# An attention and MLP kernel: a first product in three passes, another written-out order, and GpSimd additions tied to other VectorE operations

## The chip, the cores and the metric

The kernel runs on one core of one Trainium2 chip. The metric is the device time of one execution in microseconds (us); the median of three runs of the kernel before is 1144.4 us.

## What is computed

The input x has 2048 rows of 640 values. Four layers follow one another, each added to x: attention, MLP, attention, MLP, with the same weights both times.

- Attention: y = layernorm(x), qkv = y·wqkv (640×1920), 32 heads of 20 values. Each row looks at 8 rows: itself and the rows 2, 4, ..., 14 before it. Logits q·k/√20, softmax over the 8, weighted sum of v, product with wo (640×640).
- MLP: y = layernorm(x), h = gelu(y·w1 + b1) with 1536 columns, then h·w2 + b2.

```python
logits = einsum("bhsd,bhswd->bhsw", q, kg) * scale      # 8 keys a row
o = einsum("bhsw,bhswd->bhsd", softmax(logits), vg)
x = x + o @ wo
x = x + gelu(layernorm(x) @ w1 + b1) @ w2 + b2
```

## The kernel before

**Tiling.** The rows are split by parity and then in halves: four units of 512 rows, each of M = 4 tiles of 128 rows. Unit numbers 0 to 3 are the first pair of layers, 4 to 7 the second. All products are made from float16 pairs: a float32 value is split into a high half (a cast, on ScalarE) and a low half (the difference, on VectorE), and TensorE adds up three passes, high·high, high·low and low·high. The weights are scaled by 64 and split in the same way while the kernel runs; wqkv is prepared in four head groups g of three pieces (q, k, v): a ScalarE operation makes the high piece (L434), a VectorE operation the low one (L435), out of a staging buffer that a DMA has filled (L447).

**The stages of a unit.** Layer norm (for units 0 and 1 with VectorE statistics L561 to L563, a GpSimd power L566 and a VectorE scaling L606; for the others ScalarE sums, a GpSimd power L590 and ScalarE scalings); the split in high and low halves (L613 ScalarE, L615 VectorE); the transposition (by DMA, L620; for tiles 0 and 1 of unit 0 by TensorE into PSUM, L489, with a ScalarE copy back, L497); 16 products with wqkv of 15 matmuls of 480 columns (L654; tile t, head group g), each evacuated by ScalarE (L673) and stored to DRAM; then, for each head group, the gathered rows are loaded and VectorE makes products q·k (L741), sums them to logits (L745, a reduction over 20 values), softmax (L750 to L760), products with v (L767) and their sums (L775, L779). GpSimd makes the low half of the attention's output (L788). Then the product with wo (L810), the residual on VectorE (L816), the second layer norm, the addition of b2 to x on GpSimd (L624), the MLP's products (L847, L866, L869; in other forms L1024, L1061, L1124 for the last units), GELU on ScalarE, splits on VectorE (L858), residuals (L889, L1143).

**What sets the order.** The program first lists all operations with what they need, give and use (numbered in the order in which they are listed), and emits them in an order written out by hand: `ORDER` is that list of numbers. `PLACES` says which buffer of its pool each tenant gets. Each engine runs its operations in the order of emission; SyncE (SP) issues all DMAs in that order too. Waits come from the data alone, by buffers. In addition `BESIDE` names 49 GpSimd additions (L624 and L788) and for each a VectorE operation that it waits for (L1204). The `need` of an operation makes no wait by itself: it is an argument for whoever makes the order.

**Around the change.** TensorE's queue begins with nine groups of eight matmuls of 128 columns (L1153), which multiply a unit matrix with itself into a bank that nobody reads. Their listing names the first tile's statistics as a need. The product of tile 0 with head group 0 is cut into three passes of five matmuls (L661): high·high, low·high, high·low. That of tile 1 is one run of 15 (L654).

Of the kernel before, what the change touches and what calls it, by code (L numbers as in the profile page):

```python
# [261 lines left out]
def sliding_dilated_then_mlp_kernel(  # L262
# [141 lines left out]
    def identity():  # L404
# [7 lines left out]
        give=["b1"])  # L412
# [822 lines left out]
```

## Time and profile before

| | |
|---|---|
| median of 3 runs (lowest, highest) | 1144.4 us (1144.36, 1145.14) |
| profiled execution: its time, its span | 1144.26 us, 1142.5 us |
| TensorE (PE) busy | 1134.2 us, 99% |
| VectorE (DVE) busy | 1073.7 us, 94% |
| ScalarE (ACT) busy | 552.5 us, 48% |
| GpSimd (POOL) busy | 159.1 us, 14% |
| mean granted TensorE clock | 0.998 |

The span runs from the first instruction to the last; 1.76 us of the execution's time lie around it. A matmul's shown duration is longer than its share of the stream, since matmuls are pipelined: what counts for TensorE is the distance from one start to the next. The rows of the trace on which the prediction rests stand in a section of their own below. In them PE is TensorE's matmuls, PEld its weight loads, DVE VectorE, ACT ScalarE, POOL GpSimd.

### The profile page before, as it was taken

Reading aid. Unit: us, or ns where it says so; the run is one execution under the profiler, and the core shown is the slowest. Engines: PE = TensorE matmul, PEld = TensorE weight load, DVE = VectorE, ACT = ScalarE, POOL = GpSimd, SP = SyncE. Lnnn points to the kernel's source line nnn. Section 1 sums busy time; section 2 is a strip of 40 time slices with the busy share of each in tenths; the row PEclk is TensorE's granted clock in tenths of the full one; section 3 lists DMA queues with packets and bytes.
Section 4 is the critical chain, followed back from the end, with each engine's and each line's share of the span. In section 5 each row is a group of like instructions: output and inputs, shape, how many; then the busy total and the mean of one; then the engine's idle time right before and its main releaser. Section 6 shows DMA issues by size and latency. Waiting matters only on the chain.

```text
span 1142.5 us, 17648 instructions
## 1 busy us (share of the span) xinstructions
PE 1134.2 (99%) x6932; PEld 647.0 (57%) x6932; DVE 1073.7 (94%) x1003; ACT 552.5 (48%) x977; POOL 159.1 (14%) x98
## 2 busy tenths in 40 slices
PE   8999999999999999999999999999999999999998
PEld 5444446577654565445555654556455546566886
DVE  8899999999999999999999999999999999988482
ACT  5476434545364438423645552355447542286360
POOL 2011110311111113100213011121211200300000
PEclk9999999999999999999999999999999999999999
DMA  9999999899976675956475866674598877788856
GB/s 295 324 311 277 278 331 279 262 266 308 240 198 196 216 192 125 253 182 188 155 216 188 179 188 188 213 190 133 164 267 275 258 209 221 211 218 225 251 152 189
DMA packets 259023, 257.38 MB, mean 225 GB/s; under 512 B 138540, under 2 KB 209532, under 8 KB 258940
## 3 DMA queue, kind: packets, MB, share of 16 engines
q1 hardware_dynamic: 258940, 256.26, 78.0%
q8 instruction: 54, 0.88, 0.3%
q14 instruction: 29, 0.24, 0.1%
HBM read 175.64 MB, written 48.71 MB: 196 GB/s over the span
## 4 chain that ended last, share of the span: by engine, by line
PE 99%; DVE 0%; DMA 0%; issue 0%
PE ps L654 34%; PE ps L847 17%; PE acc L866 14%; PE ps L810 11%; PE acc L1124 9%; PE ps L1061 7%; PE acc L869 4%; PE acc L1024 3%; PE ps L1024 1%; PE acc L1153 0%; DMA xf<-in_A_x_dram 0%; PE ps L661 0%; DVE bn L561 0%; PE acc L489 0%; DVE hl L615 0%; DVE bn L562 0%
## 5 line engine op out<-in xcount | busy, mean ns | idle before, releaser
L654 PE MATMUL ps<-wq,yT 128*128 128x480 f16 x1905 | 390.4, 366 | 0.0
L654 PEld LDWEIGHTS <-yT 128*128 128x128 f16 x1905 | 185.6, 98 | 197.0
L847 PE MATMUL ps<-yT,c 128*128 128x512 f16 (+1 forms) x1080 | 204.0, 344 | 0.0
L866 PE MATMUL acc<-c,act 128*128 128x512 f16 x720 | 203.4, 379 | 0.0
L741 DVE TENSOR_TENSOR pr<-qk 128x2560 f32<-128x2560 f32 (+1 forms) x44 | 179.6, 4088 | 0.7
L767 DVE TENSOR_TENSOR pr<-sm,v 128x2560 f32<-128x2560 f32 (+1 forms) x44 | 177.1, 4032 | 0.4
L745 DVE TENSOR_REDUCE sm<-pr 128x128 f32<-128x2560 f32 (+1 forms) x44 | 176.6, 4017 | 0.0
L847 PEld LDWEIGHTS <-c 128*128 128x128 f16 x1080 | 103.8, 98 | 87.4
L673 ACT ACTIVATE ev<-ps 128x480 f32<-128x480 f32 x128 | 70.7, 564 | 162.9 <-PE ps L654 155.5
L869 PE MATMUL acc<-c,act 128*128 128x128 f16 x720 | 148.2, 219 | 0.0
L775 DVE TENSOR_TENSOR pr<-pr 128x2560 f32<-128x2560 f32 (+2 forms) x88 | 143.8, 1645 | 0.2
L810 PE MATMUL ps<-wo,yT 128*128 128x320 f16 x960 | 134.7, 299 | 0.0
L866 PEld LDWEIGHTS <-act 128*128 128x128 f16 x720 | 70.3, 98 | 80.3 <-DVE act L858 0.2
L810 PEld LDWEIGHTS <-yT 128*128 128x128 f16 x960 | 93.0, 98 | 38.1
L590 POOL TENSOR_TENSOR ln<-ln,half 128x2 f32<-128x2 f32 (+1 forms) x30 | 48.6, 1621 | 408.9 <-ACT ln L587 408.9
L1124 PE MATMUL acc<-c,wq 128*128 128x320 f16 x630 | 92.9, 299 | 0.0
L853 ACT ACTIVATE act<-ps,b 128x512 f32<-128x512 f32 (+1 forms) x72 | 43.8, 613 | 93.1 <-PE ps L847 56.0
L624 POOL TENSOR_TENSOR xf<-xf,b 128x640 f32<-128x640 f32 x28 | 58.1, 2085 | 172.9 <-DVE xf L816 36.0
L788 POOL TENSOR_TENSOR ohl<-o,ohl 128x640 f16<-128x640 f32 x24 | 44.3, 1846 | 266.6 <-ACT ohl L786 118.7
L1061 PE MATMUL ps<-yT,c 128*128 128x512 f16 x360 | 78.7, 379 | 0.0
L1124 PEld LDWEIGHTS <-wq 128*128 128x128 f16 x630 | 61.6, 98 | 24.2
L571 ACT ACTIVATE junk<-xf 128x640 f16<-128x640 f32 x56 | 41.1, 733 | 66.8 <-DVE xf L816 54.8
(137 smaller groups left out, 1145.1 us busy)
## 6 DMA issues: line engine op xcount, KB each, us to landing
c<-mw SPq DMA_DIRECT2D x180, 320.0 KB, 4.0
spill<-ev SPq DMA_DIRECT2D x64, 480.0 KB, 5.6
qk<-spill SPq DMA_DIRECT2D x32, 880.0 KB, 5.4
v<-spill SPq DMA_DIRECT2D x32, 880.0 KB, 5.7
c<-msp SPq DMA_DIRECT2D x36, 320.0 KB, 3.6
qk<-spill SPq DMA_DIRECT2D x32, 320.0 KB, 4.8
c<-mw SPq DMA_DIRECT2D x54, 160.0 KB, 3.1
mw<-c SPq DMA_DIRECT2D x24, 320.0 KB, 5.6
```

The costliest lines, as they stand in the source:

```text
L654: nc.tensor.matmul(ps, transposed(yk)[:, a * KD + k, t * P:(t + 1) * P], wq[:, b, k, g], start=j == 0, stop=j == 3 * KD - 1)
L673: act(3 * GC, -400 + n, lambda i=i, pk=pk, ek=ek: nc.scalar.activation(tile_of(*ek)[:, :, i], tile_of(*pk)[:, :3 * GC].rearrange("p (a c) ...
L741: return nc.vector.tensor_mul(pr(pk), w[:, HALO + m + t0:HALO + m + t0 + TH, None, :].to_broadcast([P, TH, W, GC]), windows(w, t0, [GC, W] ...
L745: dve(E, G - 0.7, lambda pk=pk, t0=t0: nc.vector.tensor_reduce(lg(t0, t0 + TH).rearrange("p t w h -> p (t w h)"), pr(pk).rearrange("p t w ...
L767: return nc.vector.tensor_mul(pr(vk).rearrange("p t w (h d) -> p t (w h) d", d=DH), lg(t0, t0 + TH).rearrange("p t w h -> p t (w h)")[:, : ...
L775: dve(TH * w * GC, G - 0.9, lambda vk=vk, w=w: nc.vector.tensor_add(pr(vk)[:, :, 0:w], pr(vk)[:, :, 0:w], pr(vk)[:, :, w:2 * w]), need=[la ...
L810: nc.tensor.matmul(tile_of(*pk)[:, :D // 2], transposed(yk)[:, a * KD + k, t * P:(t + 1) * P], wo[:, b, k, c * D // 2:(c + 1) * D // 2], s ...
L847: nc.tensor.matmul(tile_of(*pk)[:, :nt], tile_of(*ck)[:, a, k * P:(k + 1) * P], transposed(yk)[:, c * KD + k, t0 * P:t1 * P], start=i == 0 ...
L866: nc.tensor.matmul(acc[i], w, tile_of(*wk)[:, c, :BANK], start=e == 0 and (a, c) == PASS[0], stop=end, skip_group_check=True)
L869: nc.tensor.matmul(acc[4][:, i * P:(i + 1) * P], w, tile_of(*wk)[:, c, BANK:], start=e == 0 and i == t0 and (a, c) == PASS[0], stop=end, s ...
L1061: nc.tensor.matmul(tile_of(*pk), tile_of(*ck)[:, a, k * P:(k + 1) * P], transposed(yk)[:, c * KD + k, :], start=i == 0, stop=i == 3 * KD - 1)
L1124: nc.tensor.matmul(acc[bank][:, :HD], tile_of(*hk)[half][:, a, slot, t * P:(t + 1) * P], load()[:, z, c], start=q in FIRST and i == 0 and ...
```

## The change

Four edits, all of them about order and waits; no matmul, addition or transfer is added to the whole or taken from it.

1. The product of tile 1 with head group 0 in unit 0 is cut in three passes of five matmuls as well (two list entries more, so that all later numbers grow by 2).
2. The nine groups of L1153 no longer name the statistics as a need.
3. `ORDER` and `PLACES` are replaced as a whole.
4. `BESIDE` is replaced: each addition waits for another VectorE operation. In the old table the next VectorE operation after the one waited for is a sum of logits (L745) in 19 of 49 cases, in the new one in 47 of 49.

```diff
-                if n == 0 and g == 0 and t == 0:
+                if n == 0 and g == 0 and t in (0, 1):
                     def part(a, b, t=t, g=g, pk=pk):
...
-                           give=[("qkvp", n, t, g) if c else ("qkvq", a)], use=[pk, yk])
-                        last = [("qkvq", a)]
+                           give=[("qkvp", n, t, g) if c else ("qkvq", t, a)], use=[pk, yk])
+                        last = [("qkvq", t, a)]
...
     for _ in range(WARM):
-        warm([("sq", ("a", 0), 0)])
+        warm([])
...
 ORDER = """
-1 11 0 12 13 15 21 18 33 14 35 26 34 63 28 41 36 37 29 42 72 16 31 43 38 91 22 44 48 46 55 66 19 27 17 32 56 30 69 20 49 24 25 45 57 51 47 50 213 58
+0 11 1 12 13 30 15 25 28 27 21 24 32 26 84 33 29 31 18 35 34 14 41 36 37 42 91 16 44 43 69 38 22 48 46 45 55 66 49 23 56 63 50 51 19 57 53 52 39 213
...
 BESIDE = {
-    278: 298, 302: 649, 326: 163, 395: 403, 400: 538, 405: 555, 410: 724, 497: 203, 520: 533, 543: 552, 607: 778, 612: 778, 617: 802, 622: 802,
...
+    280: 135, 304: 139, 328: 342, 397: 405, 402: 2046, 407: 2128, 412: 1067, 499: 512, 522: 535, 545: 2106, 609: 781, 614: 781, 619: 802, 624: 802,
...
```

Read by engine, the two orders begin as follows (hi and lo are halves; yT is a transposed tile's copy; wqh and wql are the high and the low piece of wqkv, head group and piece; t is the tile of unit 0; "turn" a transposition on TensorE; "pass" five matmuls of L661).

```
TensorE before: 4 groups L1153, turn t0 hi, turn t0 lo, 5 groups L1153, turn t1 hi,
                pass t0 hi.hi, turn t1 lo, pass t0 lo.hi, pass t0 hi.lo, t1 (15, L654), t2, (t0, g1), t3, ...
TensorE after:  9 groups L1153, turn t0 hi, turn t0 lo, turn t1 hi, turn t1 lo,
                t0 hi.hi, t1 hi.hi, t0 lo.hi, t1 lo.hi, t0 hi.lo, t1 hi.lo, t2, (t0, g1), t3, ...
ScalarE before: hi t0, wqh 0,0, wqh 0,2, wqh 0,1, hi t2, hi t1, yT t0 hi, yT t0 lo, yT t1 hi, wqh 1,0, yT t1 lo, ...
ScalarE after:  hi t0, wqh 0,0, wqh 0,2, yT t0 hi, hi t1, hi t2, wqh 0,1, yT t1 hi, yT t1 lo, yT t0 lo, hi t3,
                wqh 1,0, wqh 1,2, wqh 1,1, ...
VectorE before: statistics t0, t1, y t0, statistics t2, lo t0, y t1, y t2, wql 0,0, wql 0,1, lo t2, lo t1, wql 0,2, statistics t3, ...
VectorE after:  statistics t0, t1, y t0, statistics t2, lo t0, y t1, y t2, wql 0,2, lo t1, lo t2, statistics t3, wql 0,0, wql 0,1,
                y t3, statistics of a tile of unit 1, lo t3, wql 1,0, wql 1,2, wql 1,1, ...
SP before:      x t0, t1, t2, w 0,0, w 0,2, w 0,1, x t3, w 1,0, w 2,0, ...
SP after:       x t0, t1, t2, w 0,0, w 0,2, w 3,1, w 0,1, x t3, ...
TensorE's end before: ..., 3 runs of "p4", "p3" mixed; last a run of p3 (tile 1); VectorE's last residual and the last output DMA follow it
TensorE's end after:  all p4 before the last five runs of p3; last the same run of p3, the same residual and output DMA
```

## Rows read from the trace of the kernel before

**Rows 1.** The page: busy us and share by engine; one group (busy us, mean ns).

```profile
PE 1134.2 (99%) x6932; PEld 647.0 (57%) x6932; DVE 1073.7 (94%) x1003; ACT 552.5 (48%) x977; POOL 159.1 (14%) x98
...
L654 PE MATMUL ps<-wq,yT 128*128 128x480 f16 x1905 | 390.4, 366 | 0.0
```

**Rows 2.** All waits of TensorE: for whom, us in total, times, longest.

```profile
PE acc L489 <- ACT hl L613: 2.8, 1, 2.8
PE acc L1153 <- POOL ident L406: 1.4, 1, 1.4
PE acc L489 <- DVE hl L615: 0.7, 1, 0.7
```

**Rows 3.** Stretches: TensorE's busy us (count), granted clock, DMA share, GB/s.

```profile
1.00:5.00 4.00, 3.60 (x32) 1.00 0.78 248
5.00:8.90 3.90, 0.45 (x5) 1.00 1.08 305
8.95:12.30 3.35, 3.32 (x32) 0.50 1.11 348
12.40:16.40 4.00, 4.00 (x39) 1.00 1.37 310
500.00:700.00 200.00, 200.00 (x1182) 1.00 0.64 182
```

**Rows 4.** Timeline of the head, TensorE: start us, us, what, count.

```profile
1.35 3.60 PE L1153 MATMUL acc<-ident 128*128 128x128 f16 x32 [1.35 <-POOL ident L406]
7.79 0.45 PE L489 MATMUL acc<-ident,hl 128*128 128x128 f16 x5 [2.84 <-ACT hl L613]
8.98 0.72 PE L489 MATMUL acc<-ident,hl 128*128 128x128 f16 x5 [0.74 <-DVE hl L615]
9.49 3.76 PE L1153 MATMUL acc<-ident 128*128 128x128 f16 x40
13.36 1.18 PE L661 MATMUL ps<-wq,yT 128*128 128x480 f16 x5
16.68 23.66 PE L654 MATMUL ps<-wq,yT 128*128 128x480 f16 x116
```

**Rows 5.** Timeline of the head, ScalarE and VectorE.

```profile
3.90 0.89 DVE L561 BATCH_NORM_STATS2 bn<-xf 128x6 f32<-128x320 f32 x2 [3.04 <-DMA xf<-in_A_x_dram]
9.13 0.87 ACT L434 ACTIVATE wq<-pr 128x800 f16<-128x800 f32 x1 [0.44 <-DMA pr<-in_A_wqkv_dram]
10.40 0.87 ACT L434 ACTIVATE wq<-pr 128x800 f16<-128x800 f32 x1 [0.40 <-DMA pr<-in_A_wqkv_dram]
11.18 1.35 ACT L613 ACTIVATE hl<-y 128x640 f16<-128x640 f32 x2
12.43 1.87 ACT L497 ACTIVATE yT<-acc 128x640 f16<-128x640 f16 x3
17.26 0.61 DVE L606 TENSOR_SCALAR y<-xf,bn 128x640 f32<-128x640 f32 x1 [0.44 <-POOL bn L566]
19.02 0.83 DVE L615 TENSOR_TENSOR hl<-y,hl 128x640 f16<-128x640 f32 x1
19.77 1.89 DVE L435 SCALAR_TENSOR_TENSOR wq<-ohl,wq 128x800 f16<-128x800 f32 x2
```

**Rows 6.** One line's instructions on GpSimd: count, min/median/max ns, first and last start.

```profile
L624 POOL TENSOR_TENSOR xf<-xf,b x28: 1536/1549/6722, 217.5 to 990.6; 128x640 f32<-128x640 f32 x28
...
L788 POOL TENSOR_TENSOR ohl<-o,ohl x24: 1387/1402/4557, 99.0 to 986.1; 128x640 f16<-128x640 f32 x24
```

**Rows 7.** Groups of VectorE by shape: count, busy us, mean ns, idle before.

```profile
L741 DVE TENSOR_TENSOR pr<-qk 128x5120 f32<-128x5120 f32 x20 | 109.8, 5489 | 0.4
...
L745 DVE TENSOR_REDUCE sm<-pr 128x256 f32<-128x5120 f32 x20 | 109.4, 5470 | 0.0
L741 DVE TENSOR_TENSOR pr<-qk 128x2560 f32<-128x2560 f32 x24 | 69.8, 2922 | 0.2
L767 DVE TENSOR_TENSOR pr<-sm,v 128x2560 f32<-128x2560 f32 x24 | 67.3, 2820 | 0.1
...
L858 DVE TENSOR_TENSOR act<-act 128x512 f16<-128x512 f32 x48 | 35.3, 737 | 0.6 <-ACT act L856 0.6
```

**Rows 8.** Timeline about two additions beside other VectorE operations.

```profile
598.38 5.48 DVE L741 TENSOR_TENSOR pr<-qk 128x5120 f32<-128x5120 f32 x1
598.54 8.68 POOL L624 TENSOR_TENSOR xf<-xf,b 128x640 f32<-128x640 f32 x2 [19.18 <-DVE sm L760]
603.78 2.03 DVE L858 TENSOR_TENSOR act<-act 128x512 f16<-128x512 f32 x1
```

**Rows 9.** Timeline at a narrow place in the middle.

```profile
358.10 0.68 DVE L858 TENSOR_TENSOR act<-act 128x512 f16<-128x512 f32 x1
...
358.83 0.10 PEld L866 LDWEIGHTS <-act 128*128 128x128 f16 x1 [0.17 <-DVE act L858]
```

**Rows 10.** Timeline of the end.

```profile
1137.83 1.25 PE L1124 MATMUL acc<-c,wq 128*128 128x320 f16 x8
...
1139.12 0.49 DVE L1143 SCALAR_TENSOR_TENSOR xf<-acc,xf 128x320 f32<-128x320 f32 x1 [0.32 <-PE acc L1124]
```

More of the change, by code (lines that the diff above doesn't have):

```diff
@@ L71 @@
 ORDER = """
[111 rows of a table removed]
[111 rows of a table added]
 """
 PLACES = """
-000000000110000110101032320001111220230203102102132000110303222011120003200121102220011202120002200001001000110100001011000001110010221012110201100111
-010110011012022101012122011201022001001000001100010010010000011001020120120002110100121210001102101202010121202111002200000100100001100100001100001101
-000102112021120011001010100011011212000121202000200112000010010000011010000100100001101012020101220011001102011101001211202021210101021210201000100100
-000110100001001000011010210201210002110001100011001102201102001222010101221020001001000001101000010010000110100012200121000111100111111000020011202120
@@ L190 @@
-101022100011200010010000011010000100100001101011220021000101111002010110011021210100220112001211201000100100000110100001001000011010220010221200212301
-132012012112000002021102002111002021102002111102020102012111002021102012111000002021102002111102020102012111002021102002111102000102112111100000020201
-020121100020211020022111010201020122111010201020022101000000101010201221100101110200221110102010201221210101010201211200000002011102002112102010102012
-112002011102112112002001102202110100000020101222120100010111222020101010101222120100010111222020001102210011102220011232100041212150001100022002100120
@@ L194 @@
-02110022100020211101021212100023211114020205100102002011020020110221100220200011010110000022220200311010140000025200211000022010010220110220
+000000000110000110101302100302111320220001112220130103020020111322020321200121102210021102210022000100100000110001000000010011000110112021210211001101
+011100110110100122210102021210102001001000000111000000100100110100012012012002011110020211011002201000121202010211120020000100100011000100100100001101
+000101212011020110011000110011002100222011120002102220000100010000011010000100100001101012121120021000110012010110011210120201012222012100122000100100
@@ new lines @@
+000110100001001000011010202010211002011001101000110011101002201120012220111000001001000001101000010010000110100120011201101010110111111000021102210021
+012200121212000010010000011010000100100001101011200021201110000102111001001201210120201110122012022000100100000110100001001000011010210121002200212301
+123012012011000001011122102010101020122112010001021122102010101020122012011000001021102002211101020102012211001021102002211101000102212211100000010001
+021122110010011022121110020001022121111020001022021101000000202010220211110201010201211200201110200211210201010201211100000002021102002211101020102012
@@ L195 @@
+211001021102102212101000102112210000000010211021021100020211020021111020101022121100020111022021002100211112000221112230001142210051001200002100100221
+00122100211120000211100022211103020224111005200112000021120000211201201020200021010111000022020200321010141000025000221001002110020021122001
 """
 BESIDE = {
[4 rows of a table removed]
[4 rows of a table added]
 }
```

226 rows, old and new, of tables (BESIDE, ORDER) are left out of this document.

## The prediction, made before the changed kernel was run

> **What bounds the kernel now.** I read the page's busy shares first: TensorE 1134.2 of 1142.5 us, VectorE 1073.7 [rows 1]. VectorE is close enough to be a suspect, so the next view is TensorE's waits. There are three in the whole execution, 4.9 us together, and all three lie before 9 us: for the unit matrix at 1.35, for the first tile's high half at 7.79, for its low half at 8.98 [rows 2, 4]. Busy time alone proves little for pipelined matmuls, so I checked the spacing. The 116 matmuls from 16.68 on take 23.66 us; the last one counts 0.366 us [rows 1], so the others start (23.66 - 0.37) / 115 = 0.203 us apart [rows 4], and 480 columns at 2.4 GHz are 0.200. The middle is as full: 200.00 of 200.00 us at clock 1.00 [rows 3]. So from the first product to the last matmul TensorE never stops, and at the end only a last residual (1139.12, 0.49 us) and its output transfer follow [rows 10]. The time is: when TensorE's dense stream begins, plus a fixed amount of work, plus this tail. VectorE's 94% is not the bound; it delivers in time, in places by little: at 358.83 a weight load follows VectorE's split with 0.17 us of idle in front of it, and the matmuls do not notice [rows 9].
>
> **Edit 1 and the new head.** No matmul comes or goes. What can change is the start of the dense stream and what lies inside it. I compare the start of tile 2's product, where both orders have done tiles 0 and 1 with head group 0. Before: 16.68 + 15 x 0.203 = 19.72 [rows 4].
>
> After, the first pass needs three high weight pieces and tile 0's high half. ScalarE's chain decides. The second piece ends at 9.13 + 0.87 = 10.00; before, ScalarE then sat idle 0.40 us until the third piece landed [rows 5]. The new order puts the copy (1.87 / 3 = 0.62) and the two casts (11.18 to 12.43, 1.25) there, so the third piece's cast starts at 10.00 + 0.62 + 1.25 = 11.87 and ends at 12.74. SP now issues one more 400 KB transfer ahead of that piece. The two pieces' casts were 10.40 - 9.13 = 1.27 us apart, each waiting for its DMA, so one transfer costs about 1.27 and the piece lands at 10.40 + 1.27 = 11.67, still in time. The first pass starts at about 12.8, not 13.36. The low half of tile 1 (0.82 on VectorE, after its cast at about 11.3) gives its transposition until 12.6, so all four transpositions lie ahead of the first pass; before, one lay between the passes. Six passes, 30 x 0.203 = 6.1, end at 18.9. That is 0.8 us sooner than 19.72.
>
> The other inputs on this path: tile 0's low copy at 12.74 + 3 x 0.62 = 14.6, wanted at 12.8 + 2 x 1.02 = 14.8. The last low weight piece: VectorE has the low halves of tiles 1 and 2 (until 13.0), a statistics group (1.3), and two pieces (1.89) [rows 5], so 16.2, wanted at 16.9. Head group 1: VectorE has 16.2 + 0.61 + 1.3 + 0.83 + 3 x 0.95 = 21.8, wanted at 18.9 + 3.05 = 21.9. All of them hold, the last by 0.1 us, so a few tenths may go there. If the extra transfer cost twice the 1.27, the piece would land at 12.94, the first pass start at 13.9 and tile 2 come 0.3 us later than before. Bounds of the head at full clock: -0.8 to +0.3; I take -0.8, since ScalarE's chain is made of rows one by one.
>
> **Edit 2 and the clock.** The dropped need is no wait: the first four groups ran at 1.35, the statistics only at 3.90 [rows 4, 5]. What the edit does is let the order put all nine groups first. Before, four ran from 1.35 to 4.95 and five from 9.49, directly ahead of the first product. The first 32 took 3.60 / 32 = 0.11 us each, which is 128 columns at 1.2 GHz (0.107). In 5.0 to 8.9 TensorE had 0.45 us of work, and the next stretch ran at granted clock 0.50, which is 1.2 GHz; after 3.4 us filled with matmuls the clock was 1.00 again at 12.4, and the first product ran at 2.4 GHz [rows 3]. So the five groups had a use: the slow time fell on them.
>
> After, 72 small matmuls run in one block from 1.35. At 0.11 us they end at 9.4; with the upper level from 4.95 on, at 4.95 + 40 x 0.053 = 7.1. From there to 12.8 TensorE has only transpositions of 0.45 us. That is a pause of 3.4 to 5.7 us; the pause that brought the clock down before lasted 4.0 (4.95 to 8.98) with one transposition in it. So I expect the first passes at 1.2 GHz, and the clock back about 3.4 us after the passes begin, as at 12.4. In 3.4 us at half speed, half is lost: 1.7 us. Bounds: 0 if the clock does not fall, and 3.2 if the rise takes as long as the first one can have taken (1.35 to 7.79 is 6.4 us, half of it lost). I take 1.7. The Trainium skill, page "TensorE: Matmul & The Clock Gate", section "Why this matters for your kernels", speaks against this edit too: idle gaps between bursts of matmuls bring the clock down. By that rule the head costs time; the trace agrees, with clock 0.50 in 8.95 to 12.30.
>
> **Edit 3, the order.** From 20 us on the work of every engine is the same and only its sequence differs. As TensorE has no wait there, a better sequence can gain nothing; a worse one can add stalls. Each is bounded by one VectorE operation ahead of the one wanted, 0.4 to 5.5 us [rows 7]; I take 0: the nearest row is the list of waits, which has none after 9 us in an order with margins as small as 0.17 us [rows 2, 9], and I could name no place in the new order where VectorE's operation is put behind its use. The end: the last run, residual and transfer are the same, the p4 outputs leave earlier; 0, by at most the 0.49 us of a residual either way [rows 10].
>
> **Edit 4, GpSimd's additions.** Alone or beside a reduction an addition takes 1.54 or 1.39 us, at most 6.72 and 4.56 [rows 6]. At 598.54 two additions beside a product and a split took 8.68 us, and the split took 2.03 instead of 0.68 [rows 8, 9]. Over the whole execution the splits lose 48 x (0.737 - 0.683) = 2.6 us and the shorter products q.k 24 x (2.922 - 2.820) = 2.4 against the same shape with v [rows 7]. With 28 fewer additions (47 - 19) beside such operations VectorE gets back some 5 us, at the most 28 x 1.35 = 38. The Trainium skill, "GPSIMD Engine Reference", section "Key points", has it that GpSimd shares its memory interfaces with VectorE and contends with operations of two inputs in that memory; a reduction has one. That rule is right here (2.03 against 0.68 us), and would be worth these microseconds if VectorE set the end. TensorE hides it: 0. What the wait costs: behind a waiting addition stand GpSimd's later additions and powers (L590), and behind a power a layer norm and the next products. In the new order 12 additions stand directly ahead of a power, 15 in the old, so I expect no more of it than before; 0, bounded by 5.5 us for one long product waited for.
>
> **Sum.** -0.8 + 1.7 + 0 + 0 = +0.9 on the profiled execution's own 1144.26 (span 1142.5 and 1.76 around it): 1145.2. The median of the runs is 1144.4, 0.14 above that execution, well inside the range.
>
> **Rivals.**
> - The clock stays up, or falls only for an instant, because the block ends late and the transpositions bridge the pause. For it: the pause could be as short as 3.4 us; against: 4.0 us with a transposition in it brought it down. Time 1144.26 - 0.8 = 1143.5. Chance 0.25.
> - Slower: GpSimd's waits cost TensorE. An addition is held for a product of 5.49 us [rows 7], the power behind it and with it a layer norm come late, the MLP's first product stands. For it: margins like 0.17 us [rows 9] and the queue in order; against: no such stall before, with as many waits. It decides from the point where TensorE waits over 1.6 us in sum after 20 us. One such stall of about 5.5 less some margin, say 4: 1145.2 + 4 = 1149. Chance 0.13.
> - VectorE was the bound after all and its 5 us come out: 1144.26 - 5 = 1139. Against it stand the three waits of rows 2. Chance 0.03.
> - The change does not do what it says: the extra transfer eats the head's gain (+0.3) and the clock falls as well: 1144.26 + 0.3 + 1.7 = 1146.3. Chance 0.09.
>
> **How the numbers follow.** The forecast, 1145.2, has 0.50. The range runs from 1142.9 (the clock stays up, with half a microsecond of luck at the end) to 1147.3 (the last rival, or the forecast with a stall of 2 us). A change of 0.2%, 2.3 us, is about what a measurement can tell from none. Faster by that needs 1142.1, which only the third rival gives: 0.04 with a remainder. Slower needs 1146.7: the stall 0.13, and a part of the last rival with a slow rise of the clock 0.03: 0.16. Same: 0.80.
>
> **What would show it.** Right: L661 starts near 12.8, its first matmuls 0.40 us apart, a granted clock of 0.50 about 13 us; tile 2's product near 20.6; TensorE's waits only in the head; splits (L858) near 0.68 in the mean, additions near 1.54 and 1.39 and no shorter time for it. Wrong: matmuls 0.20 us apart from the start (first rival), waits of TensorE on VectorE or ScalarE after 20 us (second), or a span shorter by more than the head.

## The result: 1.5 us slower, within the bound of 0.2%

The changed kernel takes 1146.45 us in the median of 22 runs (1145.44 to 1147.97), the kernel before 1144.95 (22 runs, 1144.32 to 1145.96): ratio 1.0014, 95% interval 1.0008 to 1.0020. The loss is clear of the noise, since the interval leaves out 1; it stays within the 0.2% that the prediction called no change, and inside the predicted range of 1142.9 to 1147.3. The profiled execution took 1146.4 us with a span of 1144.6, against 1144.26 and 1142.5: +2.1 us.

**The profile after.** The page's busy times of the changed kernel answer to [rows 1]: TensorE has the same matmuls, GpSimd is busy 6.4 us less, VectorE as long as before. ScalarE has two instructions more: in the new order it loads its function tables 38 times instead of 36, 1.28 us each.

```profile
PE 1136.0 (99%) x6932; PEld 646.7 (56%) x6932; DVE 1073.6 (94%) x1003; ACT 553.5 (48%) x979; POOL 152.7 (13%) x98
```

TensorE's waits of the changed kernel (us in total, times, longest) answer to [rows 2]. The last three are new and lie behind the head.

```profile
PE acc L489 <- ACT hl L613: 1.7, 1, 1.7
PE acc L1153 <- POOL ident L406: 1.4, 1, 1.4
PE acc L489 <- DVE hl L615: 1.1, 2, 0.7
PE acc L1124 <- DMA c<-msp: 0.4, 1, 0.4
PE ps L810 <- DVE xf L816: 0.2, 1, 0.2
PE ps L654 <- DMA yT<-hl: 0.2, 1, 0.2
```

TensorE's head after, and below it the stretches with the granted clock (columns as in [rows 3, 4]):

```profile
1.35 6.45 PE L1153 MATMUL acc<-ident 128*128 128x128 f16 x72 [1.35 <-POOL ident L406]
...
12.66 7.92 PE L661 MATMUL ps<-wq,yT 128*128 128x480 f16 x30
20.42 9.88 PE L654 MATMUL ps<-wq,yT 128*128 128x480 f16 x48
```

```profile
5.00:8.90 3.90, 3.25 (x45) 1.00 1.05 300
8.95:12.30 3.35, 1.06 (x13) 1.00 1.09 361
13.00:16.30 3.30, 3.30 (x10) 0.50 1.68 307
16.40:19.80 3.40, 3.40 (x18) 1.00 0.75 217
```

The first pass starts at 12.66, but 10 matmuls fill 13.00 to 16.30 at a granted clock of 0.50, that is 1.2 GHz, where 16 would fit at 0.203 us each. So tile 2's product starts at 20.42 instead of 19.72: the head costs 0.70 us against this execution of the kernel before. The old start is not that early in every execution, as experiments 3 and 11 show.

The other 1.4 us of the span come later, at places where the distance between two starts exceeds the usual one, each given by the start that is late: by 0.33 us at 290.88 (a transposition by DMA lands late), 0.37 at 780.74 and 0.59 at 1055.96, 1.29 together, and by 0.15 at 252.7. Behind 20 us the kernel before has no distance that is more than 0.12 us too long. The second place, in VectorE's timeline and TensorE's:

```profile
774.81 5.48 DVE L745 TENSOR_REDUCE sm<-pr 128x256 f32<-128x5120 f32 x1
780.21 0.48 DVE L816 SCALAR_TENSOR_TENSOR xf<-ps,xf 128x320 f32<-128x320 f32 x1
...
780.74 1.52 PE L810 MATMUL ps<-wo,yT 128*128 128x320 f16 x10 [0.21 <-DVE xf L816]
```

The new order has put a residual, which frees the bank that the next product with wo wants, directly behind a sum of logits of 5.48 us. In the kernel before a residual stood behind such a sum too, at 777.17, but TensorE did not wait there. The third, in SP's queue and TensorE's:

```profile
1050.76 1.24 SPq L536 DMA_TRANSPOSE yT<-hl  x1
...
1055.96 0.58 PE L1124 MATMUL acc<-c,wq 128*128 128x320 f16 x3 [0.43 <-DMA c<-msp]
```

The weights for this matmul are in the last of the four transfers that SP issued just ahead, and directly behind them a transposition is issued at 1050.76. That this one slows the transfer is a reading of the order, not shown: here the slowest of these transfers lands 5.7 us after its issue, while in experiment 2 below, with the same order in the queue, the same transfer lands 4.1 us after it and TensorE does not wait there.

The additions on GpSimd and the VectorE groups beside them, after (columns as in [rows 6, 7]):

```profile
L624 POOL TENSOR_TENSOR xf<-xf,b x28: 1537/1544/1819, 217.7 to 1031.4; 128x640 f32<-128x640 f32 x28
L788 POOL TENSOR_TENSOR ohl<-o,ohl x24: 1393/1401/5937, 101.4 to 986.4; 128x640 f16<-128x640 f32 x24
```

```profile
L741 DVE TENSOR_TENSOR pr<-qk 128x2560 f32<-128x2560 f32 x24 | 67.5, 2819 | 0.2
...
L858 DVE TENSOR_TENSOR act<-act 128x512 f16<-128x512 f32 x48 | 32.1, 682 | 0.6 <-ACT act L856 0.5
```

The longest addition of L624 falls from 6.72 to 1.82 us, the split's mean from 737 to 682 ns and the shorter product's from 2922 to 2819. Of the 52 additions 36 ran mainly beside a sum of logits before (the line with the longest overlap), 47 do now. The longest addition of L788, beside a product with v, grows from 4.56 to 5.94 us. The collisions are largely gone, and the time does not follow. VectorE's busy time does not fall either, though the splits and products give back the 5 us that were forecast. Other groups rise, L779 (128x640) from 812 to 888 ns in the mean; the rest of the difference was not followed.

### The profile page after: what moved, and what is told of

It reads as the page before. It is cut to its first block, busy times and chain, and to the rows that moved or that the text cites. A ratio compares the mean times of both kernels' runs of the same rounds, so it can differ in the third digit from the quotient of the medians.

```text
span 1144.6 us, 17585 instructions
## 1 busy us (share of the span) xinstructions
PE 1136.0 (99%) x6932; PEld 646.7 (56%) x6932; DVE 1073.6 (94%) x1003; ACT 553.5 (48%) x979; POOL 152.7 (13%) x98
## 4 chain that ended last, share of the span: by engine, by line
PE 86%; DVE 9%; issue 2%; DMA 2%; POOL 0%; ACT 0%; SPq 0%; DVEq 0%; ACTq 0%
PE ps L654 29%; PE ps L847 14%; PE acc L866 11%; PE ps L810 11%; PE acc L1124 8%; PE ps L1061 7%; PE acc L869 3%; PE acc L1024 3%; DVE pr L741 2%; DVE sm L745 2%; DVE pr L767 2%; DVE pr L775 1%; PE ps L661 1%; DMA yT<-hl 1%; DMA pr<-in_A_wqkv_dram 1%
## 5 line engine op out<-in xcount | busy, mean ns | idle before, releaser
L741 DVE TENSOR_TENSOR pr<-qk 128x2560 f32<-128x2560 f32 (+1 forms) x44 | 177.2, 4032 | 0.5
L745 DVE TENSOR_REDUCE sm<-pr 128x128 f32<-128x2560 f32 (+1 forms) x44 | 176.8, 4020 | 0.1
L866 PEld LDWEIGHTS <-act 128*128 128x128 f16 x720 | 70.2, 98 | 79.6
L590 POOL TENSOR_TENSOR ln<-ln,half 128x2 f32<-128x2 f32 (+1 forms) x30 | 61.3, 2044 | 358.4 <-ACT ln L587 358.4
L1124 PE MATMUL acc<-c,wq 128*128 128x320 f16 x630 | 93.6, 299 | 0.4 <-DMA c<-msp 0.4
L788 POOL TENSOR_TENSOR ohl<-o,ohl 128x640 f16<-128x640 f32 x24 | 39.7, 1655 | 315.2 <-ACT ohl L786 118.6
L1124 PEld LDWEIGHTS <-wq 128*128 128x128 f16 x630 | 61.6, 98 | 25.2 <-DMA c<-msp 0.8
L869 PEld LDWEIGHTS <-act 128*128 128x128 f16 x720 | 68.2, 98 | 8.1
```

Of the source, the lines that this page charges most:

```text
L741: return nc.vector.tensor_mul(pr(pk), w[:, HALO + m + t0:HALO + m + t0 + TH, None, :].to_broadcast([P, TH, W, GC]), windows(w, t0, [GC, W] ...
L745: dve(E, G - 0.7, lambda pk=pk, t0=t0: nc.vector.tensor_reduce(lg(t0, t0 + TH).rearrange("p t w h -> p (t w h)"), pr(pk).rearrange("p t w ...
L866: nc.tensor.matmul(acc[i], w, tile_of(*wk)[:, c, :BANK], start=e == 0 and (a, c) == PASS[0], stop=end, skip_group_check=True)
L869: nc.tensor.matmul(acc[4][:, i * P:(i + 1) * P], w, tile_of(*wk)[:, c, BANK:], start=e == 0 and i == t0 and (a, c) == PASS[0], stop=end, s ...
L1124: nc.tensor.matmul(acc[bank][:, :HD], tile_of(*hk)[half][:, a, slot, t * P:(t + 1) * P], load()[:, z, c], start=q in FIRST and i == 0 and ...
```

## The experiments

Each was timed against the kernel before on the same chip. The list numbers 24 to 32 are the nine groups of L1153.

**1. The nine groups first, in the old order.** Only the clock's part of the change, without anything else of it.

```diff
-... 16 31 43 38 91 22 44 48 46 55 66 19 27 17 32 56 30 69 20 49 24 25 45 ...
+... 16 31 24 25 27 30 32 43 38 91 22 44 48 46 55 66 19 17 56 69 20 49 45 ...
```

> The kernel before with one thing changed: all nine groups of L1153 stand ahead of the first transposition, as in the changed kernel. Theory (the clock): TensorE pauses from about 7.8 us to the first product, the granted clock falls to 0.50 about there and comes back some 3.4 us later; the first product starts a little earlier than 13.36, since no group stands in front of it, but the matmuls run 0.40 us apart for a while; tile 2's product starts at 20.3 to 21.1 instead of 19.72, the span is 0.6 to 1.4 us longer, no wait of TensorE after 20 us. Rival (the groups have no use): clock 1.00 at the first product, tile 2's product at 19.3 to 19.7, span the same or up to 0.4 us shorter.

Measured: 1145.69 us (11 runs) against 1144.72 (33), ratio 1.0009 (1.0001 to 1.0018), no wait of TensorE after 20 us. Its head and a stretch of it:

```profile
13.49 2.18 PE L661 MATMUL ps<-wq,yT 128*128 128x480 f16 x5
...
19.21 7.05 PE L654 MATMUL ps<-wq,yT 128*128 128x480 f16 x34
```

```profile
12.40:16.40 4.00, 3.50 (x16) 0.50 1.35 318
11.60:18.30 6.70, 5.40 (x21) 0.50 1.17 274
```

The first five matmuls take 2.18 us instead of 1.18, tile 1's product starts at 19.21 instead of 16.68, and the span, 1145.0 us, is longer by the same 2.5. The profiled execution is the longest of the eleven. Its clock stays at 0.50 for some 6.8 us (second line), twice as long as in the changed kernel's profile. In the median the loss is 1.0 us, so the price differs between executions.

**2. The changed kernel with its pause filled**: five more groups of L1153 between and behind the transpositions, their result unused.

```diff
-... 16 44 43 69 38 22 48 46 45 55 66 49 23 56 63 50 51 19 ...
+... 16 44 30 43 69 38 22 48 46 30 30 30 45 55 66 49 23 56 63 50 51 30 19 ...
```

> The changed kernel with five more groups of L1153 in the pause: one after tile 0's high transposition, three after its low one, one after tile 1's high one (40 small matmuls that nobody reads). Theory (the clock costs the head 1.7 us): the clock stays at 1.00, first pass at 12.7, 30 matmuls 0.203 us apart, tile 2's product at 18.7 to 19.0 instead of 20.42; span 1.5 us under the changed kernel's (1144.6), so 1143.1, if its three small waits in the middle (0.2 to 0.4 us each) come again. Rival 1: the clock falls all the same, tile 2 at 20.4. Rival 2: the groups hold up the transpositions of tile 1 and the first pass starts after 13.0.

Measured: 1145.57 (11 runs) against 1144.72, ratio 1.0009 (1.0000 to 1.0018); span 1142.7. Its head:

```profile
13.08 6.24 PE L661 MATMUL ps<-wq,yT 128*128 128x480 f16 x30
19.15 7.05 PE L654 MATMUL ps<-wq,yT 128*128 128x480 f16 x34
```

The 30 matmuls take 6.24 us instead of 7.92, and tile 2 starts 0.57 us sooner than before. The theory had 0.7 to 1.0: the first pass starts at 13.08, which is the sign named for the second rival, but ahead of it tile 1's transposition waits 1.21 us for ScalarE and not for the added groups. The median stays 0.85 above before: something behind the head costs more than the head gives. In this profile that is 0.80 us, of it 0.38 at 779.12 (L816 again) and 0.34 at 1126.94 (weights of L1124). In ten of the eleven runs the mean granted clock is 1.000, and these ten still spread from 1144.51 to 1148.49.

**3. The rule of the waits alone**, in the old order: 30 of the 49 additions wait for the VectorE operation just ahead of the next sum of logits.

```diff
-    278: 298, 302: 649, 326: 163, 395: 403, 400: 538, 405: 555, 410: 724, 497: 203, ...
+    278: 865, 302: 314, 326: 478, 395: 515, 400: 538, 405: 2136, 410: 2196, 497: 368, ...
```

> The kernel before, its order untouched; only the table of GpSimd's waits follows the new rule: 30 of the 49 additions now wait for the VectorE operation just ahead of the next sum of logits, which is 1 to 10 operations later. Theory (TensorE bounds, VectorE's saving is hidden): additions nearly all at 1.54 and 1.39 us, their longest under 3, splits L858 near 0.68 us in the mean (0.737 before), and the span within 0.3 us of 1142.5. Rival 1 (VectorE sets the pace): span 3 to 5 us shorter. Rival 2 (the waits hold GpSimd's powers and TensorE with them): waits of TensorE after 20 us, span 1 us or more longer.

Measured: 1144.62 (11 runs) against 1144.72, ratio 1.0001 (0.9992 to 1.0010). GpSimd's busy time falls to 140.7 us and VectorE's to 1069.4; TensorE waits only in the head. Its span, 1143.2, is 0.7 us longer than before, and all of that is the head: tile 1's product starts at 17.38 instead of 16.68, so tile 2's at 17.38 + 15 x 0.203 = 20.42, as late as in the changed kernel, although nothing in the old start is changed. The 40 small matmuls run at the pace of 1.2 GHz to their end here (4.47 us instead of 3.76).

```profile
9.28 4.47 PE L1153 MATMUL acc<-ident 128*128 128x128 f16 x40
...
17.38 7.86 PE L654 MATMUL ps<-wq,yT 128*128 128x480 f16 x38
```

The collisions go in part (the split's mean is 709 ns, where 0.68 us was expected, and the longest additions are 4.1 and 4.5 us, not under 3), VectorE gets back 4.3 us, and no gain can be told from none. Neither rival shows: the time is not 3 us shorter, and no wait comes behind 20 us.

**4. The changed kernel again**, unaltered, in the same set of runs as the first three.

> The changed kernel once more, unaltered: does the fall of the clock in the head recur, and do the three waits in the middle (at 290, 780 and 1055 us)? Theory (the order has three places without margin): tile 2's product at 20.2 to 20.8 again, waits of TensorE at the same places, 0.2 to 0.6 us each, span 1144.2 to 1145.2. Rival (they were an accident of one execution): waits elsewhere or none, span under 1143.6. Timed: 1.0 to 2.0 us above the kernel before.

Measured: 1146.62 (11 runs), ratio 1.0019 (1.0011 to 1.0028); tile 2 at 20.70, span 1144.5. The fall of the clock recurs (the 30 matmuls take 7.92 us again). Of the three late waits those for L816 (0.2 us) and for the weights of L1124 (0.5) come back; the one at 290 does not.

**5 and 6. The new head up to tile 2's product, then the old order, places and waits; without and with the five groups of experiment 2.** The new list is kept to number 222.

```diff
-... 62 2 67 222 71 220 87 216 68 81 419 227 ...
+... 62 2 67 222 78 81 216 68 71 79 87 413 ...
```

> The changed kernel's head (product of tile 1 in three passes, its order up to tile 2's product) and behind it the kernel before's order, buffers and GpSimd waits. Theory (the head costs 0.7 to 1 us by the clock, the new middle the rest): clock 0.50 about the first passes, tile 2's product at 20.2 to 20.8, no wait of TensorE after 30 us, span 1143.0 to 1143.6, median 0.5 to 1.0 us above the kernel before. Rival (the new middle costs nothing on the whole): as slow as the changed kernel, 1.5 us above.

> The same with five more groups of L1153 in the pause. Theory: clock 1.00, tile 2's product at 18.8 to 19.2 against 19.72 before, no wait after 30 us, span 1141.7 to 1142.1, median 0.5 to 0.9 us under the kernel before: the new head alone is worth its 0.8 us once the clock is held up. Rival (the earlier start is given back, because the later head groups' weights come no sooner): waits of TensorE for wq between 20 and 40 us, median level with the kernel before.

Measured: 1148.5 (5 runs), ratio 1.0035 (1.0023 to 1.0048), and 1150.13 (median; one of the five took 6383 and is not in the ratio), ratio 1.0046 (1.0032 to 1.0059). Both medians miss their theories by far, since the joint itself makes a stall. The first fence shows TensorE's wait in experiment 5, the clock behind it and ScalarE's wait; the second shows experiment 6:

```profile
28.16 22.09 PE L654 MATMUL ps<-wq,yT 128*128 128x480 f16 x100 [2.07 <-ACT ev L673]
...
28.60:31.90 3.30, 3.30 (x10) 0.50 0.53 168
...
25.49 0.87 ACT L434 ACTIVATE wq<-pr 128x800 f16<-128x800 f32 x1 [4.48 <-DMA pr<-in_A_wqkv_dram]
```

```profile
18.80 6.24 PE L654 MATMUL ps<-wq,yT 128*128 128x480 f16 x30
29.09 21.15 PE L654 MATMUL ps<-wq,yT 128*128 128x480 f16 x91 [4.06 <-ACT ev L673]
...
29.10:34.30 5.20, 5.20 (x14) 0.50 0.40 122
```

ScalarE's evacuations stand behind casts of weights in the old list, and the joint brings those weights later: the cast for which they wait starts at 25.49 and in experiment 6 at 26.44, against 20.92 in the kernel before. So the head that ends 1.05 us sooner (tile 2 at 18.80 instead of 19.85) gains nothing. The wait is not the whole price, because the clock falls behind it: 10 matmuls in 3.30 us, and 14 in 5.20. The late starts between 28 and 35 us add up to 3.8 and 6.8 us; behind 35 us only one distance, in experiment 5, is over 0.12 us too long (0.16). Apart from the joint, then, the old middle costs next to nothing.

**7. Two of the late places mended**, with the five groups: the residual of 780 ahead of the long sum, the transposition of 1050 behind two more weight transfers.

```diff
-... 1661 1538 1553 1657 1391 ... 1393 1390 1655 ...
+... 1661 1538 1390 1553 1657 1391 ... 1393 1655 ...
-... 1960 1843 3224 ... 1850 3229 3249 3220 ...
+... 1960 3224 ... 1850 3229 3249 1843 3220 ...
```

> The changed kernel with the five groups in the pause and two operations moved: a residual of unit 5 (L816), whose product is ready 10 us before, ahead of the sum of logits of 5.48 us at 774.81 instead of behind it; and a DMA transposition of the last unit (L536) behind the next two weight loads instead of in front of them. Theory (these are the two steady stalls of the new order): no wait at 780 and none at 1055, span 0.4 to 1.0 us under that with the groups alone (1142.7, median 1145.6), run-to-run spread smaller. Rival (the stalls move on): waits at later places of the same sum.

Measured: 1145.95 (11 runs) against 1144.89, ratio 1.0011 (1.0002 to 1.0020). The waits of this run:

```profile
PE acc L1024 <- DMA c<-mw: 1.4, 1, 1.4
...
PE ps L654 <- ACT ev L673: 0.8, 1, 0.8
PE ps L654 <- DMA yT<-hl: 0.8, 1, 0.8
```

At both mended places the wait is gone (the distances are still 0.20 and 0.18 us too long), and others take over, at 25.24, 38.40 and 1071.07 us, as the rival has it. The theory's "two steady stalls" were not so steady: in experiment 2 the one at 1055 had not come. The head of experiment 7 was the earliest of all (first pass at 12.04, tile 2 at 18.22), and the two waits at 25 and 38 give 1.6 us of it back. The mending is not shown to be worth anything.

**8. The changed kernel without any of the waits.**

```diff
 BESIDE = {
-    280: 135, 304: 139, 328: 342, 397: 405, 402: 2046, 407: 2128, 412: 1067, ...
-    ...
 }
```

> The changed kernel without any of the 49 waits of GpSimd's additions, so that each runs as soon as its data are there. Theory (the waits neither help nor harm TensorE): the three small waits in the middle are there as in the changed kernel, additions up to 4 to 7 us and splits L858 above 0.70 us in the mean, span within 0.5 us of 1144.6, median 1.2 to 2.2 us above the kernel before. Rival 1 (the waits cause the stalls): no waits of TensorE in the middle, span 1 us shorter. Rival 2 (the waits protect VectorE and so TensorE): more waits, span 1 us or more longer.

Measured: 1166.82 (5 runs), ratio 1.0194 (1.0176 to 1.0211): 20 us more than the changed kernel. TensorE's two largest waits and one group of this run:

```profile
PE acc L866 <- DVE act L858: 7.5, 7, 2.0
PE ps L810 <- DVE xf L816: 4.2, 5, 1.8
```

```profile
L858 DVE TENSOR_TENSOR act<-act 128x512 f16<-128x512 f32 x48 | 39.3, 830 | 0.5 <-ACT act L856 0.5
```

The second rival holds. VectorE's busy time rises by 22 us, to 1095.7, and TensorE waits for VectorE at many places. Behind the wait of 2.0 us at 411.79 the clock falls as well, to 0.50 until 415.97. So in the new order it matters much that the additions wait. That it does not matter which table they wait by is shown for the old order alone, and for the rule of experiment 3.

**9. The new start, then the old rest.** Where the two orders have emitted exactly the same set of 664 entries (at 222 us) the list passes from the new order to the old, with the old waits (four additions of the start keep the new ones) and, by a renaming of buffers, the old places.

```diff
 (behind entry 664)
-919 1995 913 2031 2004 530 2005 525 410 ...
+1995 913 2031 2004 2005 410 919 525 ...
```

> The changed order for the first 664 list entries (some 222 us, a point at which both orders have sent out exactly the same work), then the order and the waits of before, with the buffers of before in the rest. Theory (clock in the head plus stalls in the middle that come with the new order of the rest): granted clock 0.50 about 13 us, tile 2's product at 20.2 to 20.8, no wait of TensorE after 225 us, span 1143.2 to 1143.9, median 0.5 to 1.0 us above the kernel before. Rival A (all of the loss is the head's, the stalls are chance): median 1.3 us or more above, as the changed kernel. Rival B (the head costs nothing over many runs): within 0.2 us of before.

Measured: 1144.87 (11 runs) against 1144.78 (33), ratio 1.0001 (0.9992 to 1.0010), span 1142.8. Its head, and a stretch of it:

```profile
12.97 7.23 PE L661 MATMUL ps<-wq,yT 128*128 128x480 f16 x30
20.04 4.21 PE L654 MATMUL ps<-wq,yT 128*128 128x480 f16 x20
```

```profile
12.00:14.90 2.90, 2.75 (x13) 0.50 1.13 361
```

No wait follows the head. The clock falls here too, but earlier against the work (0.50 from 12 to 15 us), so that only 0.99 us is lost instead of 1.68, and tile 2 starts 0.32 later than before. The theory had 0.5 to 1.0 in the median; it came out 0.09 above, as the second rival had it (a head that costs next to nothing over many runs). The interval, 0.9 us below to 1.1 above, does not exclude the theory.

**10. The same with the pause filled** by the five groups (the edit of experiment 2).

> The same, with five more groups of eight small matmuls of the first statistics kind in the pause ahead of the first product (their result isn't used). Theory: granted clock 1.00 from 5 us on, the first 30 matmuls in 6.2 us, tile 2's product at 18.3 to 19.2, span 1141.7 to 1142.5, median 0.3 to 0.9 us below the kernel before and 1.2 to 1.7 below the kernel with the new start alone; small waits of TensorE between 24 and 40 us may give some of it back. Rival (a head that ends sooner only meets waits for the weights and statistics behind it): waits of 0.8 us or more between 20 and 45 us, and a median within 0.3 us of before.

Measured: 1144.54 (11 runs) against 1144.78, ratio 1.0001 (0.9992 to 1.0010); span 1142.8. The clock stays at 1.00, and:

```profile
13.29 6.24 PE L661 MATMUL ps<-wq,yT 128*128 128x480 f16 x30
19.36 4.82 PE L654 MATMUL ps<-wq,yT 128*128 128x480 f16 x23
```

Tile 2 starts 0.36 us sooner than before, less than the theory had, and a late start by 0.37 us at 1002.88 (a wait for ScalarE) and one by 0.24 at 278.14 use it up. Both lie in the old order, which has no late start when its own head runs before it. The median stands 0.24 below before, which the interval does not tell from none; no version here is shown to beat the kernel before.

**11. The old start, then the new rest with its waits**: the complement of experiment 9. Tile 1's product is listed in three passes here, one behind the other.

```diff
 (behind entry 664, against the kernel before with its numbers grown by 2)
-1995 913 2031 2004 2005 410 919 525 ...
+919 1995 913 2031 2004 530 2005 525 410 ...
```

> The other half: the order of before for the first 664 entries, then the changed order with its waits. Theory (stalls in the middle belong to the changed order): head as before, tile 2's product at 19.6 to 20.0, waits of TensorE of 0.4 to 2 us in sum after 225 us, at about 780 and 1055 us among them, median 0.5 to 1.2 us above before. Rival (the head alone is the loss): no waits after 9 us and a median within 0.2 us of before.

Measured: 1145.80 (11 runs) against 1144.78, ratio 1.0010 (1.0001 to 1.0019). Span 1144.8, with two late waits and more long distances, 1.7 us of them together behind 222 us; the head is 0.6 us late in this one execution: tile 2's product starts at 20.32, with the old start, as in experiment 3.

```profile
PE ps L654 <- DMA yT<-hl: 0.5, 1, 0.5
...
PE ps L810 <- DVE xf L816: 0.2, 1, 0.2
```

The late starts are by 0.69 us at 291.27, 0.38 at 781.14, 0.27 at 1056.03 and 0.26 at 236.66. So the places at 290, 780 and 1055 belong to the new order of the rest, and that alone makes 1.0 us in the median (interval 0.1 to 2.2).

**12. Experiment 1 with seven more groups in its pause.**

```diff
-... 22 44 48 46 55 66 ...
+... 22 44 30 48 46 30 30 30 30 30 30 55 66 ...
```

> The kernel before with all nine groups of the first statistics ahead of the first transposition (as in the first experiment) and seven more such groups in the pause ahead of the first product (result not used). Theory (what that experiment lost is the clock): granted clock 1.00 in 12.4 to 16.4, the first five matmuls of the head's product in 1.1 us instead of 2.18, tile 1's product at 17.2 to 18.2 instead of 19.21, median 0.7 to 1.3 us below that experiment's 1145.69 less what the chip differs, so within 0.3 us of the kernel before. Rival (what it lost is the order of VectorE and ScalarE behind the moved groups): median still 0.6 us or more above before, with the clock up.

Measured: 1144.36 (11 runs) against 1144.78, ratio 1.0000 (0.9991 to 1.0009), span 1142.5, clock 1.00 throughout:

```profile
13.38 1.19 PE L661 MATMUL ps<-wq,yT 128*128 128x480 f16 x5
...
16.71 7.45 PE L654 MATMUL ps<-wq,yT 128*128 128x480 f16 x36
```

The head is that of the kernel before again, and the median is 1.33 us below experiment 1 (by each one's own before: 1.39). With the same order, the pause ahead of the first product is the whole loss, as far as intervals of about 1 us can tell. The Trainium skill, "TensorE: Matmul & The Clock Gate", section "Why this matters for your kernels", says that idle gaps between bursts of matmuls bring the clock down. By that rule the two traces agree: 0.50 in 12.40 to 16.40 with the gap, 1.00 with it filled.

## Why the number was right, and which step was not

The forecast was 1145.2 us, 0.9 above its base of 1144.26; the median came out at 1146.45. About half of the miss of 1.25 us lies in the base: the median of the kernel before is 1144.4 in the three runs known then and 1144.95 in 22. The change itself is +1.5 instead of +0.9, in the profiles +2.1.

- What bounds: right. TensorE's stream is dense from its start on in both kernels, and the time is its start, its work and the few tenths where it stands.
- Edit 1, the head at full clock: right in its path. ScalarE's third cast was forecast at 11.87 and starts at 11.76, the first pass at 12.8 and starts at 12.66; where the clock stays up (experiment 2) tile 2 follows the first pass by the 6.1 us that were forecast. The gain of 0.8 us is less sure than its rows made it look: with the pause filled tile 2 came 0.57, 0.92, 1.50 and 0.36 us sooner than before in experiments 2, 6, 7 and 10.
- Edit 2, the clock: the fall and its price are right in this execution, 7.92 - 6.24 = 1.68 us against 1.7. The forecast of the net, +0.9, measured +0.70. Too sure was that this is a fixed price: depending on when the clock falls it was 0.99 in experiment 9, and over many runs the new start costs 0.1 us, with an interval of about 1 us either way. What the step left out is that the old start pays too: the profile from which I took 19.72 is a favourable one, and with the same start tile 2 came at 20.42 and 20.32 in experiments 3 and 11, about as late as in the changed kernel (20.42 and 20.70).
- Edit 3, the order, taken at 0: this is the step that failed, by its size. In the rest alone it costs 1.0 us (experiment 11, 0.1 to 2.2), in the profile of the changed kernel 1.4. The bound in the text, one VectorE operation ahead of the one wanted, was the right mechanism for the wait at 780. For the one at 1055, where TensorE waits for a transfer of weights, the prediction had no term. I took 0 because I could name no place, although the narrow place of [rows 9] had shown how little slack there is anywhere. The premise that the work of every engine stays the same was off by ScalarE's two table loads, but no new wait of TensorE is for ScalarE. Nor did the bound reckon with the clock, which falls behind a stall of 2 us (experiments 5 and 8); here the stalls were shorter and it did not.
- Edit 4, GpSimd's waits, taken at 0: right as far as experiment 3 tests it, with the new rule in the old order. The table itself changes less than its description says: 12 of the 49 additions keep the operation that they wait for, and the "28 fewer" are counted from the table, where the traces show 11 more additions beside a sum (36 and 47 of 52). The reason, that TensorE hides it, holds for the 5 us that were at stake and not much further: 22 us more on VectorE came out as 20 us (experiment 8).
- The rivals: a clock that stays up did not come; the passes that would show it are those of experiments 2 and 10. GpSimd's waits stalled nothing that shows: none of the three late waits is for it, and the power (L590) ahead of the late transposition at 290 starts 0.63 us later than before, no more than the head's 0.70. The extra transfer cost the head nothing.

So that the forecast came out near is in part luck: the range is 4.4 us wide, and the sum's two terms were off in opposite ways. By the medians the head costs less than 0.9 us and the order more than 0. The parts, 0.1 (experiment 9) and 1.0 (experiment 11), add up to 1.1 of the 1.5 to 1.9 that the changed kernel loses; the difference is within the intervals. That the clock adds something in the changed kernel is seen in the traces of experiments 2 and 4 (30 matmuls in 6.24 and 7.92 us); their medians lie 1.05 us apart, with intervals that overlap. What stays open is why experiment 7, without the known waits, is no faster than experiment 2: its new waits are known, why they come just there is not.

## What to carry to other kernels

In a stream that never stops, a new order of everything is not free where the profile shows no slack: cost it at a few tenths for each place that is narrow, and look first for operations that free a bank and stand behind a long one. A stall of some 2 us can cost nearly as much again, when the clock falls behind it (experiment 5). Matmuls without a use may have one: look at what the clock did after the last pause ahead of the first product before you move them. Contention taken from an engine off the path is worth nothing until it fills that engine's slack; how much slack there is shows by taking the protection away, not by the busy share.

## What was not expected of the hardware

- The price of the same pause varies between executions and kernels: the 30 matmuls behind it took 7.92 us (the changed kernel, twice), 7.34 (experiment 5) and 7.23 (experiment 9), and 6.24 with the pause filled. Even the kernel before parts by its clock: of its 81 runs beside the experiments, the 23 with a mean granted clock of 0.998 have a median of 1144.17 us, the 38 with 1.000 one of 1144.88 and the 12 with 0.997 one of 1145.51. The execution from which the prediction started, 1144.26, is of the first kind. (A mean of 1.000 does not mean that the clock was up from the start; the last but one point says why.)
- In the middle of the dense stream a short wait can bring the clock down. Behind waits of 2.07 us (experiment 5) and 2.02 (experiment 8, at 411.79) it stood at 0.50 for 3.4 us. Behind two others of experiment 8, of 1.92 and 1.78 us, it did not fall. Why these differ is open.
- The granted clock in the rows and the spacing of the matmuls do not always agree: in experiment 11 the stretch 8.95 to 12.30 is shown at 1.00, while the 40 small matmuls from 9.26 on take 4.47 us, 0.11 each, the pace of 1.2 GHz. The trace has no record of the clock there: its first one begins at 13.86 us, and a stretch without a record is shown as 1.00. In the kernel before the first begins at 5.50, so the 1.00 of the first stretch in [rows 3] says nothing, and the spacing of 0.11 us decides. The spacing has to be read beside the clock at the start of a trace.

```profile
9.26 4.47 PE L1153 MATMUL acc<-ident 128*128 128x128 f16 x40
```

```profile
8.95:12.30 3.35, 3.35 (x34) 1.00 1.11 347
```

- In the new order the waits in the table hold off 20 us (experiment 8), by far more than the 5 us of collisions that were left in the kernel before.
